# A linear-attention and expert kernel: attention units overlapped three deep in a written VectorE order, with filling products on TensorE

## The chip, the core and the metric

One core of a Trainium2 chip runs the whole program. It has five engines with a queue each: TensorE (PE in the profile; its weight loads are PEld), VectorE (DVE), ScalarE (ACT), GpSimd (POOL) and SyncE (SP, which here only issues transfers). The metric is the device time of one execution in microseconds (us).

## The reference

Three stages follow one another; the token rows pass from each to the next.

```python
# 1  attention: 4 batches x 8 heads, 768 steps, head size 48
for t in range(S):
    state = alpha[t, :, None] * state + outer(k[t], v[t])
    y[t] = q[t] @ state
x = y as 3072 rows of 384
# 2  experts: each token goes to one of 8 (argmax of a normalised product with expert_emb)
expert_idx = argmax(xn @ en.T / tau);  gate_w = its softmax probability
x = gate_w * (relu(x @ w1[e]) @ w2[e])          # 384 -> 1024 -> 384
# 3  a second network on all tokens
h = x @ w_in;  out = max(0.01 * h, h) @ w_out   # 384 -> 2048 -> 384
```

## The kernel before

**Attention** works on 16 units; unit i is one batch and one pair of heads, with the heads on partitions 0 to 47 and 64 to 111 and time along the free axis, cut into 12 chunks of 64 steps. `unit(i)` does, in dependency order:

- VectorE scans alpha forward into `bc`, the decay from each chunk's start (L326); takes 12 reciprocals as seeds (L328); scans alpha backwards into `rc`, the inverse decays (L333); and multiplies k by them into `kh` (L335). GpSimd multiplies q by `bc` into `qb` (L329), ScalarE spreads the chunk decays into `en` (L331).
- TensorE transposes `kh` in six blocks (L352), which ScalarE copies to `kn` (L355); forms the scores of all chunks, `kh` with `qb` (L343); VectorE multiplies them by a triangular mask into `am` (L346).
- TensorE forms each chunk's sum of k and v (L367); VectorE scans these into the carried states `st` (L371). TensorE then adds `am` with v (values, L385) and `qb` with `st` (carried, L392) in `py`, and ScalarE copies the result rows to `xb` (L401).

**Routing** follows for each batch once its four units are done: `columns` transposes the rows (L448) and takes the products with the experts' embeddings (L460, 8 columns each), `squares` sums the squares of the rows, and `route` goes through about 25 operations on 128x6 or 128x48 tiles on VectorE, ending in `slot`. Then GpSimd scatters the batch's rows into per-expert buckets in DRAM with six indirect transfers (L532). The buckets are first cleared by `zero_rows` (L539, L540), on SP's queue. The scattered rows of the last batch are what the first expert gathers (L745).

What sets the order is the class `Plan`: every operation is added with an engine, an assumed duration, what it reads and writes, and a wish time `at`. `order` lists them greedily by assumed start, and `emit` issues them in that order, so each engine has a fixed queue and runs it strictly in order. The weights of the first expert are split into two fp16 parts in the same plan (L563 on ScalarE, L564 on VectorE). `fence` is a TensorE drain.

**The experts and the second network** (from L616 on) are not planned but written out; before the first expert, `x2h` and `x2l`, the second network's input, are set to zero by VectorE (L620) and GpSimd (L621).

## Time and profile before

| | |
|---|---|
| median of 3 runs | 897.55 us (897.52 to 908.74) |
| the profiled execution | 898.16 us, span 896.4 us |
| TensorE, VectorE, ScalarE, GpSimd busy | 782.0, 461.2, 361.1, 152.5 us |
| mean granted TensorE clock | 0.88 |
| first scan, last key product ends, last scatter begins, first expert product | 13.3, 201.4, 234.8, 253.1 us |

The span has two parts. From 13.3 to 253 us the attention and the routing run, with TensorE mostly at half of its clock; from 253 us on the products of the experts and of the second network fill TensorE at nearly its full clock. The profile gives each engine's busy time by stretch, the granted clock as a share of full speed (0.50 is 1.2 GHz, 1.00 is 2.4 GHz), and a timeline of single instructions. Ends of matrix products are modelled and overlap the next one's start, so where one row follows another directly, the step from start to start is the better price.

### The profile page before, as it was taken

Reading aid. Unit: us, or ns where it says so; the run is one execution under the profiler, and the core shown is the slowest. Engines: PE = TensorE matmul, PEld = TensorE weight load, DVE = VectorE, ACT = ScalarE, POOL = GpSimd, SP = SyncE. Lnnn points to the kernel's source line nnn. Section 1 sums busy time; section 2 is a strip of 40 time slices with the busy share of each in tenths; the row PEclk is TensorE's granted clock in tenths of the full one; section 3 lists DMA queues with packets and bytes.
Section 4 is the critical chain, followed back from the end, with each engine's and each line's share of the span. In section 5 each row is a group of like instructions: output and inputs, shape, how many; then the busy total and the mean of one; then the engine's idle time right before and its main releaser. Section 6 shows DMA issues by size and latency. Waiting matters only on the chain.

```text
span 896.4 us, 17082 instructions
## 1 busy us (share of the span) xinstructions
PE 782.0 (87%) x7172; PEld 476.2 (53%) x7172; DVE 461.2 (51%) x748; ACT 361.1 (40%) x661; POOL 152.5 (17%) x130
## 2 busy tenths in 40 slices
PE   1839989889288798788698999999999999999996
PEld 1738878788244344344354445545546446455453
DVE  5668686781356666665667673062260350540620
ACT  2235242422136665765666343152251340531520
POOL 3011231212313222322324000100000001001001
PEclk9656576665579899999899999999999999999999
DMA  9975453201275859768766000000000000000000
GB/s 309 329 251 167 130 179 108 93 2 55 71 194 174 167 138 228 168 149 235 153 156 207 15 2 10 27 1 18 19 1 19 18 1 27 10 10 24 3 10 28
DMA packets 63729, 87.56 MB, mean 98 GB/s; under 512 B 29848, under 2 KB 42912, under 8 KB 63648
## 3 DMA queue, kind: packets, MB, share of 16 engines
q1 hardware_dynamic: 41472, 72.27, 28.3%
q10 hardware_dynamic: 19040, 4.65, 3.1%
q0 software_dynamic: 3136, 9.50, 2.8%
q8 instruction: 58, 0.95, 0.5%
q14 instruction: 23, 0.19, 0.1%
HBM read 66.85 MB, written 14.91 MB: 91 GB/s over the span
## 4 chain that ended last, share of the span: by engine, by line
issue 40%; PE 24%; DVE 13%; DMA 12%; ACT 6%; POOL 4%; ACTq 1%; SPq 0%; POOLq 0%; DVEq 0%
DMA wstage<-in_w_out 5%; DMA xt<-xs 4%; PE py L385 4%; PE pkv L367 3%; PE pkv L460 3%; POOL out L728 3%; PE py L392 2%; PE ptr L352 2%; PE psc L343 2%; ACT wstage L187 2%; DVE t L641 2%; PE ptr L448 1%; DVE w2l L194 1%; DVE rc L333 1%; ACT w2h L189 1%
## 5 line engine op out<-in xcount | busy, mean ns | idle before, releaser
L711 DVE SCALAR_TENSOR_TENSOR g<-ps,r 128x512 f32<-128x512 f32 x96 | 65.7, 685 | 150.3 <-ACT r L710 150.3
L723 PE MATMUL ps<-woh,gh 128*128 128x384 f16 x384 | 125.2, 326 | 0.0
L725 PE MATMUL ps<-woh,gl 128*128 128x384 f16 x384 | 125.2, 326 | 0.0
L724 PE MATMUL ps<-wol,gh 128*128 128x384 f16 x384 | 125.2, 326 | 0.0
L705 PE MATMUL ps<-x2h,wih 128*128 128x512 f16 x288 | 109.2, 379 | 0.0
L707 PE MATMUL ps<-x2h,wil 128*128 128x512 f16 x288 | 109.2, 379 | 0.0
L706 PE MATMUL ps<-x2l,wih 128*128 128x512 f16 x288 | 109.2, 379 | 0.0
L715 DVE TENSOR_TENSOR gl<-g,gh 128x512 f16<-128x512 f32 x96 | 66.5, 693 | 64.1 <-ACT gh L714 64.0
L714 ACT ACTIVATE gh<-g 128x512 f16<-128x512 f32 x96 | 60.4, 630 | 83.8 <-DVE g L711 83.8
L695 PE MATMUL ps<-hl,w2h 128*128 128x432 f16 x192 | 69.7, 363 | 15.4 <-DVE hl L686 15.3
L728 POOL DMA_INDIRECT out<-osb,tki x24 | 23.3, 971 | 350.9 <-ACT osb L727 344.1
L680 PE MATMUL ps<-xt,w1h 128*128 128x432 f16 x192 | 67.5, 351 | 12.5 <-DVE hl L686 12.1
L727 ACT ACTIVATE osb<-ps,ms 128x384 f32<-128x384 f32 x24 | 13.9, 580 | 159.5 <-PE ps L725 159.5
L694 PE MATMUL ps<-hh,w2h 128*128 128x432 f16 x192 | 69.6, 363 | 8.1 <-ACT hh L685 7.9
L696 PE MATMUL ps<-hh,w2l 128*128 128x432 f16 x192 | 69.6, 362 | 0.0
L681 PE MATMUL ps<-xt,w1h 128*128 128x432 f16 x192 | 67.5, 351 | 0.1
L682 PE MATMUL ps<-xt,w1l 128*128 128x432 f16 x192 | 67.4, 351 | 0.0
L710 ACT ACTIVATE r<-ps 128x512 f32<-128x512 f32 x96 | 55.9, 582 | 8.3 <-PE ps L707 8.3
L352 PE MATMUL ptr<-ident,kh 128*128 128x128 f32 x96 | 23.3, 409 | 35.2 <-DVE kh L335 34.6
L192 POOL TENSOR_TENSOR w1l<-wstage,w1h 128x768 f16<-128x768 f32 x21 | 34.7, 1653 | 109.6 <-ACT w1h L189 109.6
L724 PEld LDWEIGHTS <-gh 128*128 128x128 f16 x384 | 37.6, 98 | 25.1
L723 PEld LDWEIGHTS <-gh 128*128 128x128 f16 x384 | 37.6, 98 | 25.1
(181 smaller groups left out, 1293.1 us busy)
## 6 DMA issues: line engine op xcount, KB each, us to landing
wstage<-in_w SPq DMA_DIRECT2D x64, 384.0 KB, 5.1
a<-in_aT SPq DMA_DIRECT2D x16, 390.5 KB, 3.4
q<-in_qT SPq DMA_DIRECT2D x16, 384.0 KB, 4.2
k<-in_kT SPq DMA_DIRECT2D x16, 384.0 KB, 5.3
wstage<-in_w_in SPq DMA_DIRECT2D x16, 384.0 KB, 3.1
wstage<-in_w_out SPq DMA_DIRECT2D x16, 384.0 KB, 5.2
bucket<-zero SPq DMA_DIRECT2D x8, 582.0 KB, 7.8
v<-in_v SPq DMA_DIRECT2D x8, 576.0 KB, 8.8
```

The costliest lines, as they stand in the source:

```text
L680: nc.tensor.matmul(ps, w1h[:, k, fs], xth[:, k], start=k == 0, stop=False)
L681: nc.tensor.matmul(ps, w1h[:, k, fs], xtl[:, k], start=False, stop=False)
L682: nc.tensor.matmul(ps, w1l[:, k, fs], xth[:, k], start=False, stop=k == KD - 1)
L694: nc.tensor.matmul(ps, w2h[:, f, dsl], hh, start=f == 0, stop=False)
L695: nc.tensor.matmul(ps, w2h[:, f, dsl], hl, start=False, stop=False)
L696: nc.tensor.matmul(ps, w2l[:, f, dsl], hh, start=False, stop=f == NF1 - 1)
L705: nc.tensor.matmul(ps, wih[:, k, fs], xh[:, k], start=k == 0, stop=False)
L706: nc.tensor.matmul(ps, wih[:, k, fs], xl[:, k], start=False, stop=False)
L707: nc.tensor.matmul(ps, wil[:, k, fs], xh[:, k], start=False, stop=k == KD - 1)
L723: nc.tensor.matmul(ps, ghs[f][:, ts], woh[:, f], start=f == 0, stop=False)
L724: nc.tensor.matmul(ps, ghs[f][:, ts], wol[:, f], start=False, stop=False)
L725: nc.tensor.matmul(ps, gls[f][:, ts], woh[:, f], start=False, stop=f == NF2 - 1)
```

## The change

`unit(i)` is taken apart into `front` (scans, key product, query product, transposes), `score`, `mask_scores`, `middle` (values, then sums) and `back` (state scan, carried, rows). One round of the loop puts down the front and the scores of unit i, the mask of unit i-1, the back of unit i-2 and the middle of unit i-1. `in_turn` chains these VectorE operations, so the planner can't reorder them among each other. The scaled query no longer has a tile: it is written over `rc` after the key product has read it, so it waits for that product; `rc` and `en` have three buffers. Two drains per unit are gone. The last unit's query product is on VectorE, and its result stands in the scores' bank.

`emit` now puts products of 512 columns of ones (`keep_busy`) wherever the plan leaves TensorE a gap, into a bank that is free then; 15 stand ahead of everything. 73 more are in gaps.

The routing of a batch is spread over three rounds; that of the third batch is put behind the last unit, as are the last four weight pieces. The squares of the last batch are summed on VectorE in three parts. Only rows 256 to 431 of each expert's bucket are cleared, later; `x2h` and `x2l` are not cleared. The loads' order changes with the plan.

```diff
-    HOP = 0.2
+    HOP, TAIL = 0.07, {"PE": 0.2}
...
+    def add(self, eng, us, fn, reads=(), writes=(), pe=(), ps=(), lock=False, at=None, size=0, after=()):
+        deps = {self.wrote[k] for k in after}
...
+    def emit(self, keep=None, banks=(), us=0.22, share=0.6):
...
+        pe = [i for i in order if self.ops[i][0] == "PE"]
+        for i, j in zip(pe, pe[1:]):
+            t0, t1 = self.start[i] + self.ops[i][1], self.start[j]
...
+            if free:
+                t0, b = min(free)
+                due += [(t0 + n * us, 0, lambda b=b: keep(b)) for n in range(int((t1 - t0) * share / us + 0.4))]
+        for _, _, fn in sorted(due, key=lambda d: d[:2]):
+            fn()
...
+        tbc, trc = tiles_of("bc", [AW], 2), tiles_of("rc", [AW], 3)
+        tkh, tam = tiles_of("kh", [S], 2), tiles_of("am", [2, NC, CL], 2)
+        tkn, ten, tst = tiles_of("kn", [NC, P], 2), tiles_of("en", [HD, NCL], 3), tiles_of("st", [HD, NCL], 2)
...
+        busy = tiles_of("busy", [512], 1, F16)[0]
+        nc.vector.memset(busy, 1.0)
...
-            plan.add(G_, 1.76, lambda: nc.gpsimd.tensor_tensor(chunks(qb), chunks(q), bcv[:, :, 1:W], op=ALU.mult),
-                     [("q", i % 3), ("bc", i % 2)], [("qb", i % 3)], lock=True)
...
+        def in_turn(us, fn, reads, writes, ps=(), lock=False):
+            plan.add(V, us, fn, reads, writes, ps=ps, lock=lock, after=["turn"] if "turn" in plan.wrote else ())
+            plan.wrote["turn"] = len(plan.ops) - 1
...
+        def front(i):
+            a, q, k = ta[i % 3], tq[i % 3], tk[i % 3]
+            bc, rc, kh, kn, en = tbc[i % 2], trc[i % 3], tkh[i % 2], tkn[i % 2], ten[i % 3]
+            bcv, rcv = chunks(bc, 0, W), chunks(rc, 1, W)[:, :, 1:]
+            in_turn(1.76, lambda: nc.vector.tensor_tensor_scan(bc, a, onesP, 0.0, op0=ALU.mult, op1=ALU.add), [("a", i % 3)], [("bc", i % 2)], lock=True)
+            in_turn(0.2, lambda: nc.vector.reciprocal(seeds[:, W::W], bcv[:, :, CL]), [("bc", i % 2)], ["seeds"])
...
+            in_turn(1.76, lambda: nc.vector.tensor_tensor_scan(rc[:, ::-1], a[:, ::-1], seeds[:, ::-1], 0.0, op0=ALU.mult, op1=ALU.add),
+                    [("a", i % 3), "seeds"], [("rc", i % 3)], lock=True)
+            in_turn(0.94, lambda: nc.vector.tensor_tensor(chunks(kh), chunks(k), rcv, op=ALU.mult), [("k", i % 3), ("rc", i % 3)], [("kh", i % 2)], lock=True)
+            if i < NU - 1:
+                plan.add(G_, 1.76, lambda: nc.gpsimd.tensor_tensor(rcv, chunks(q), bcv[:, :, 1:], op=ALU.mult),
+                         [("q", i % 3), ("bc", i % 2)], [("rc", i % 3)], lock=True)
+            else:
+                in_turn(0.94, lambda: nc.vector.tensor_tensor(rcv, chunks(q), bcv[:, :, 1:], op=ALU.mult), [("q", i % 3), ("bc", i % 2)], [("rc", i % 3)], lock=True)
...
+                            nc.tensor.matmul(psc[CL * p:CL * p + CL, j, cp * CL:(cp + 1) * CL], kh[r, t], rcv[r, 2 * cp + p], start=True, stop=True)
+            plan.add(T_, 0.7, scores, [("kh", i % 2), ("rc", i % 3)], ["sc"], pe=SCB)
...
+        def part_squares(b, h, n, row):
+            x, w = txb[b % 3][:, :, 2 * h * HD:2 * (h + n) * HD], late[:, :, :2 * n * HD]
+            small(S_, lambda: nc.scalar.activation(w, x, AF.Square), [("xb", b % 3, u, g) for u in range(h, h + n) for g in range(2)], ["late"], 0.2 + 0.48 * n)
+            small(V, lambda: nc.vector.tensor_reduce(tsm[b % 2][:, row], w, AX.X, ALU.add), ["late"], [("part", h)], 0.1 + 0.6 * n)
...
-                         [("bucket", b, c)], size=P * AUG * 4, lock=True)
+                         [("bucket", b, c)], size=P * AUG * 4)
...
-                nc.sync.dma_start(bucket[e * NT:e * NT + 384].rearrange("(n p) d -> p n d", p=P), zero.unsqueeze(1).to_broadcast([P, 3, AUG]))
-                nc.sync.dma_start(bucket[e * NT + 384:e * NT + CAP], zero[:CAP - 384])
-            plan.add(Q_, 0.16, go, [], [("zeroed", e)], size=CAP * AUG * 4)
+                nc.sync.dma_start(bucket[e * NT + z0:e * NT + z0 + P], zero)
+                nc.sync.dma_start(bucket[e * NT + z0 + P:e * NT + CAP], zero[:CAP - z0 - P])
+            plan.add(Q_, 0.16, go, [], [("zeroed", e)], size=(CAP - z0) * AUG * 4, after=["turn"])
...
-            for i in range(NU):
+            for i in range(NU + 2):
                 plan.at = i
                 if i + 2 < NU:
                     load(i + 2)
-                unit(i)
+                if i < NU:
+                    front(i)
+                if 1 <= i <= NU:
+                    mask_scores(i - 1)
+                if i < NU:
+                    score(i)
+                if i >= 2:
+                    back(i - 2)
+                if 1 <= i <= NU:
+                    middle(i - 1)
...
-                    zero_rows(2 * i - 2)
-                    zero_rows(2 * i - 1)
+                if 2 <= i < 6:
+                    zero_rows(2 * i - 4)
+                    zero_rows(2 * i - 3)
...
-                if i >= 4 and i % 4 < 2:
-                    for c in range(3 * (i % 4), 3 * (i % 4) + 3):
-                        columns(i // 4 - 1, [c], range(KD))
-                        squares(i // 4 - 1, c)
-                    if i % 4 == 1:
-                        plan.at = i + 0.8
-                        route(i // 4 - 1, False)
-                if i == NU - 2:
+                b, step = divmod(i - 6, NP)
+                if 0 <= b < B - 1 and step < 3:
+                    for c in range(2 * step, 2 * step + 2):
+                        columns(b, [c], range(KD))
+                        squares(b, c)
+                    if step == 2:
+                        plan.at = i + 0.8 if b < B - 2 else NU + 1.2
+                        route(b, False)
+                if i == NU - 1:
+                    plan.at = NU - 0.2
+                    part_squares(B - 1, 0, 2, 0)
+                if i == NU:
+                    plan.at = NU + 0.5
                     for c in range(0, NC, 2):
                         columns(B - 1, [c, c + 1], range(KD - 1))
-                    for c in range(NC):
-                        squares(B - 1, c, 2 * (NP - 1) * HD)
+                    part_squares(B - 1, 2, 1, 11)
                     small(S_, lambda: nc.scalar.activation(lga, spare(0, 1), AF.Copy), [("dots", 1, 0, c) for c in range(NC)], ["lga"], 0.25, ps=KVB)
-                if 7 <= i < 15:
-                    convert(i - 7, *pieces[i - 7], w_first)
+                if 8 <= i < 16:
+                    plan.at = NU + 1 if i > 11 else i
+                    convert(i - 8, *pieces[i - 8], w_first)
+            plan.at = NU + 1.5
             columns(B - 1, [0, 1, 2], [KD - 1])
             columns(B - 1, [3, 4, 5], [KD - 1], V)
+            part_squares(B - 1, 3, 1, 12)
             route(B - 1, True)
-            plan.emit()
+            def keep_busy(bank):
+                nc.tensor.matmul({"s0": psc[:, 0], "t0": ptr[0], "t1": ptr[1]}[bank], ones16, busy, start=True, stop=True)
+            for _ in range(15):
+                keep_busy("s0")
+            plan.emit(keep_busy, ("s0", "t0", "t1"))
...
-    nc.vector.memset(x2h.rearrange("p k t -> p (k t)").bitcast(F32), 0.0)
-    nc.gpsimd.memset(x2l.rearrange("p k t -> p (k t)").bitcast(F32), 0.0)
```

**VectorE, a middle unit.** Before, units 4 and 5 (`bc` forward decays, `rc` inverse decays, `kh` scaled keys, `am` masked scores, `st` states, `sm` routing):

```order
L335 TENSOR_TENSOR kh_124<-k_109,rc_119 128x768
L326 SCALAR_TENSOR_TENSOR bc_117<-a_104,onesP_98 128x781
L328 RECIPROCAL seeds_99<-bc_117 128x12
L333 SCALAR_TENSOR_TENSOR rc_119<-a_104,seeds_99 128x781
L346 TENSOR_TENSOR am_126<-psc,mask_100 128x768
L371 SCALAR_TENSOR_TENSOR st_132<-pkv,en_130 128x576
L335 TENSOR_TENSOR kh_123<-k_110,rc_119 128x768
L326 SCALAR_TENSOR_TENSOR bc_118<-a_105,onesP_98 128x781
L328 RECIPROCAL seeds_99<-bc_118 128x12
L333 SCALAR_TENSOR_TENSOR rc_119<-a_105,seeds_99 128x781
L346 TENSOR_TENSOR am_125<-psc,mask_100 128x768
```

Now, the same place:

```order
L345 SCALAR_TENSOR_TENSOR bc_117<-a_104,onesP_98 128x781
L346 RECIPROCAL seeds_99<-bc_117 128x12
L349 SCALAR_TENSOR_TENSOR rc_120<-a_104,seeds_99 128x781
L351 TENSOR_TENSOR kh_122<-k_110,rc_120 128x768
L387 TENSOR_TENSOR am_125<-psc,mask_100 128x768
L425 SCALAR_TENSOR_TENSOR st_131<-pkv,en_130 128x576
L345 SCALAR_TENSOR_TENSOR bc_118<-a_105,onesP_98 128x781
L346 RECIPROCAL seeds_99<-bc_118 128x12
L349 SCALAR_TENSOR_TENSOR rc_121<-a_105,seeds_99 128x781
L351 TENSOR_TENSOR kh_123<-k_111,rc_121 128x768
L387 TENSOR_TENSOR am_124<-psc,mask_100 128x768
```

The mask stood behind the next unit's second scan or ahead of the key product, as the plan had it; now every round reads scan, reciprocal, scan, key product, mask of the unit before, states of the one before that.

**TensorE, a middle unit without routing.** Before (`ptr` transposes, `psc` scores, `pkv` sums, `py` values and carried):

```order
L352 MATMUL ptr_160<-ident,kh_124 128x128 x3
L352 MATMUL ptr_161<-ident,kh_124 128x128 x3
L343 MATMUL psc<-qb_120,kh_124 64x64 x24
L367 MATMUL pkv<-v_112,kn_128 48x24 x44
L385 MATMUL py<-v_112,am_126 64x48 x24
L392 MATMUL py<-st_132,qb_120 64x48 x22
L352 MATMUL ptr_160<-ident,kh_123 128x128 x3
```

Now (`busy` and `ones` are the filling products):

```order
L360 MATMUL ptr_160<-ident,kh_122 128x128 x3
L360 MATMUL ptr_161<-ident,kh_122 128x128 x3
L666 LDWEIGHTS ones_75
L666 MATMUL psc<-busy_175,ones_75 128x512
L666 LDWEIGHTS ones_75
L666 MATMUL psc<-busy_175,ones_75 128x512
L373 MATMUL psc<-rc_120,kh_122 64x64 x24
L432 MATMUL py<-st_131,rc_121 64x48 x22
L666 LDWEIGHTS ones_75
L666 MATMUL ptr_160<-busy_175,ones_75 128x512
```

Between the transposes and the scores stand two filling products; the carried products are of the unit two back, and behind them stand three filling products (the first is the last row here), then values and sums of the unit before. In a round with routing, its transposes and 8-column products stand there, with at most a few filling ones.

**GpSimd, the end of attention.** Before:

```order
L329 TENSOR_TENSOR qb_120<-q_106,bc_117 128x768
L329 TENSOR_TENSOR qb_121<-q_107,bc_118 128x768
L329 TENSOR_TENSOR qb_122<-q_108,bc_117 128x768
L329 TENSOR_TENSOR qb_120<-q_106,bc_118 128x768
L532 DMA bucket<-xb_116,slot_149 24576x388 x6
L532 DMA bucket<-xb_114,slot_150 24576x388 x6
L621 MEMSET x2l 128x5256
```

Now:

```order
L353 TENSOR_TENSOR rc_120<-q_107,bc_118 128x12x64
L575 DMA bucket<-xb_115,slot_150 24576x388 x6
L353 TENSOR_TENSOR rc_121<-q_108,bc_117 128x12x64
L575 DMA bucket<-xb_116,slot_149 24576x388 x6
L575 DMA bucket<-xb_114,slot_150 24576x388 x6
L209 TENSOR_TENSOR w1l<-wstage,w1h 128x768 x3
```

The last query product is gone from this queue (it is on VectorE), the second batch's scatters stand two query products later, and `x2l` is not cleared. The third and fourth batch's scatters close the attention on this queue as before.

## Rows read from the trace of the kernel before

**Rows 1.** Busy time by stretch; columns: stretch, length, five engines, PEclk, DMA, GB/s.

```profile
...
13.30:201.40 188.10, 152.54 (x3608) 137.11 (x3609) 142.82 (x173) 65.27 (x131) 38.79 (x28) 0.64 0.51 168
201.40:234.80 33.40, 26.93 (x390) 24.09 (x387) 9.75 (x39) 8.52 (x25) 5.85 (x6) 0.50 0.10 37
234.80:253.10 18.30, 2.64 (x12) 2.28 (x13) 7.55 (x14) 2.67 (x6) 10.29 (x7) 0.50 0.59 193
98.00:111.50 13.50, 13.31 (x231) 12.12 (x234) 8.05 (x21) 3.07 (x7) 3.62 (x3) 0.50 0.38 126
```

**Rows 2.** VectorE's groups, 13.3 to 201.4: line, operation, count, busy, mean ns, idle before.

```profile
...
L333 DVE TENSOR_TENSOR_SCAN rc<-a,seeds 128x781 f32<-128x781 f32 x16 | 46.2, 2888 | 0.5
L326 DVE TENSOR_TENSOR_SCAN bc<-a,onesP 128x781 f32<-128x781 f32 x16 | 28.4, 1776 | 0.0
L371 DVE TENSOR_TENSOR_SCAN st<-pkv,en 128x576 f32<-128x576 f32 x14 | 18.9, 1351 | 12.3 <-PE pkv L367 10.9 <-ACT junk L466 1.4
...
L346 DVE TENSOR_TENSOR am<-psc,mask 128x768 f32<-128x768 f32 x15 | 14.2, 948 | 21.7 <-PE psc L343 21.7
...
L503 DVE SCALAR_TENSOR_TENSOR cand<-lg,em 128x48 f32<-128x48 f32 x3 | 0.6, 208 | 0.1
```

**Rows 3.** Timeline at 182.5: start, duration, engine, line, operation, idle before.

```profile
...
182.57 1.68 POOL L329 TENSOR_TENSOR qb<-q,bc 128x768 f32<-128x768 f32 x1 [8.44 <-DVE bc L326]
182.74 3.16 DVE L333 TENSOR_TENSOR_SCAN rc<-a,seeds 128x781 f32<-128x781 f32 x1
```

**Rows 4.** Timeline at 107.4, GpSimd and VectorE.

```profile
...
107.41 1.68 POOL L329 TENSOR_TENSOR qb<-q,bc 128x768 f32<-128x768 f32 x1 [10.43 <-PE pkv L367]
107.53 1.35 DVE L371 TENSOR_TENSOR_SCAN st<-pkv,en 128x576 f32<-128x576 f32 x1
```

**Rows 5.** Timeline of TensorE, 86 to 98.

```profile
...
86.95 1.56 PE L343 MATMUL psc<-qb,kh 48*64 48x64 f32 x48
88.29 2.38 PE L367 MATMUL pkv<-v,kn 64*48 64x24 f32 x88
...
91.43 3.13 PE L385 MATMUL py<-v,am 64*64 64x48 f32 x48
94.67 1.52 PE L392 MATMUL py<-st,qb 48*64 48x48 f32 x44
96.12 1.54 PE L448 MATMUL ptr<-ident,xb 128*128 128x128 f32 x6
```

**Rows 6.** Timeline of TensorE, 174 to 184.

```profile
...
174.24 1.87 PE L385 MATMUL py<-v,am 64*64 64x48 f32 x47
...
176.69 1.24 PE L392 MATMUL py<-st,qb 48*64 48x48 f32 x44
177.86 0.87 PE L448 MATMUL ptr<-ident,xb 128*128 128x128 f32 x6
178.57 2.07 PE L460 MATMUL pkv<-enT,xt 128*128 128x8 f32 x18
180.50 0.85 PE L352 MATMUL ptr<-ident,kh 128*128 128x128 f32 x6
181.28 0.93 PE L343 MATMUL psc<-qb,kh 48*64 48x64 f32 x48
182.03 1.50 PE L367 MATMUL pkv<-v,kn 64*48 64x24 f32 x88
```

**Rows 7.** Timeline of TensorE at 600, products of 512 columns.

```profile
...
600.19 0.38 PE L707 MATMUL ps<-x2h,wil 128*128 128x512 f16 x1
600.40 0.38 PE L705 MATMUL ps<-x2h,wih 128*128 128x512 f16 x1
```

**Rows 8.** Timeline between the last scatter and the first expert.

```profile
...
236.09 0.96 POOL L532 DMA_INDIRECT bucket<-xb,slot  x1 [0.30 <-issue]
...
245.25 4.44 DVE L620 MEMSET x2h<- 128x5256 f32 x1 [8.87 <-issue]
...
247.77 0.62 ACT L664 ACTIVATE xs<-xg 128x384 f32<-128x384 f32 x1 [15.18 <-DMA xg<-bucket]
```

More of the change, by code (lines that the diff above doesn't have):

```diff
@@ L98, in order @@
             free[eng] = t + us
-            end[i] = t + us
+            end[i] = t + us + self.TAIL.get(eng, 0.0)
             if size:
@@ L117, in order @@
         return sorted(done, key=lambda i: start[i])
-    def emit(self):
-        for i in self.order():
-            self.ops[i][2]()
+    def emit(self, keep=None, banks=(), us=0.22, share=0.6):
+        order = self.order()
+        due = [(self.start[i], 1, self.ops[i][2]) for i in order]
+        held = {b: sorted([(self.start[i], "w") for i in order if b in self.ops[i][4]] + [(self.end[i], "r") for i in order if b in self.ops[i][5]]) for b in banks}
+        pe = [i for i in order if self.ops[i][0] == "PE"]
+        for i, j in zip(pe, pe[1:]):
+            t0, t1 = self.start[i] + self.ops[i][1], self.start[j]
+            free = []
+            for b in banks:
+                last = [h for h in held[b] if h[0] < t1]
+                if not last:
+                    free.append((t0, b))
+                elif last[-1][1] == "r":
+                    free.append((max(t0, last[-1][0] + 0.1), b))
+            if free:
[3 more added lines that the diff above has]
+            fn()
 BLK = 512
@@ new lines, in middle, with values @@
+        def middle(i):
+            b, hp = divmod(i, NP)
+            vt, am, kn = tv[b % 2], tam[i % 2], tkn[i % 2]
+            _, key, banks = result(i)
+            def values():
+                for cp in range(NC):
+                    for j in range(2):
+                        for p in range(2):
+                            r, e0 = slice(CL * p, CL * p + CL), (2 * hp + j) * HD
+                            nc.tensor.matmul(y_of(i, 2 * cp + p, j), am[r, j, cp], vt[r, cp, e0:e0 + HD], start=cp == 0, stop=False)
+            plan.add(T_, 1.4, values, [("am", i % 2), ("v", b % 2, hp // 2)], [key], pe=banks)
```

117 lines of the change are left out of this document (47 added, 70 removed).

## The prediction

> **What bounds the kernel now.** I read the busy time by stretch first [rows 1]. The reader is to see three stretches ahead of the experts: 188.1 us from the first scan to the last key product, 33.4 us to the last batch's scatter, 18.3 us to the first expert product. In the first one VectorE works 142.8 us and TensorE 152.5, and neither sets the pace alone: VectorE stands still for 188.1 - 142.8 = 45.3 us, and its groups say for what [rows 2]: 21.7 us at the mask for the scores, 10.9 at the state scan for the sums, both TensorE's. TensorE is late because its granted clock is 0.64 there and 0.50 in the next stretch [rows 1]. So I read TensorE's timeline at both levels. At 1.2 GHz one unit takes 1.54 (transposes; the same six as the routing's row), 1.34 (scores, start to start), 2.38 (sums), 3.24 (values), 1.45 (carried) = 9.95 us [rows 5]. At 2.4 GHz it takes 0.78 + 0.75 + 1.50 + 1.87 + 1.17 = 6.07 us [rows 6]. The second loss is on VectorE itself: the backward scan takes 2.89 us in the mean, the forward one of the same size 1.78 [rows 2]. The timeline shows why: GpSimd's query product starts 0.17 us ahead of the backward scan, runs 1.68, and the scan lasts 3.16 [rows 3].
>
> Everything behind the first expert product is unchanged, so the sum needs only those three stretches. It is made against the profiled execution, 898.16 us, which is 0.6 us above the median of the runs shown.
>
> **First stretch, VectorE.** The query product now follows the key product, so beside it run the mask and the state scan. A state scan beside that very GpSimd product took 1.35 us, as its mean, and the product its 1.68 [rows 4, 2]: no price. A mask beside it is in no row; bounds are nothing (the state scan's row) and a full block of 1.68 per unit; I take nothing, since it reads PSUM as the state scan does. So 16 x (2.888 - 1.776) = 17.8 us go. Up to the last key product VectorE also loses one mask (0.95), one state scan (1.35), four low weight parts (128x768 as the mask, 0.95 each) and some 24 routing operations of 0.21 [rows 2] to the last stretch: 11.1 us. 142.8 - 17.8 - 11.1 = 113.9; the ends of these operations overlap a little, so less than their means go, and I take 116, or 7.25 per round.
>
> **First stretch, TensorE.** If it held 2.4 GHz: 15 units x 6.07 = 91; 14 routing groups of three transposes (half of 0.71) and three products (0.107 each) = 9.5 [rows 6]; 64 filling products in that stretch at 0.21, the step of two products of 512 columns [rows 7] = 13.4. Together 114 us, just under VectorE's 116. At 1.2 GHz: 15 x 9.95 = 149; 14 x (0.77 + 0.64, doubling the products) = 20; 64 x 0.42 = 27; together 196 us, far over it. Two drains a unit are gone, which I don't deduct. So the clock decides, and the filling products are what the change offers for it.
>
> Which level will it be? From 98.0 to 111.5 TensorE was busy 13.31 of 13.50 us, and the clock stayed at 0.50 [rows 1]; from 174 to 183 it ran at its full level through transposes, scores, values, carried and sums [rows 6]. Being occupied is thus not enough, and the attention's own products can hold the level once it is there. Products of 512 columns stand now between these in seven rounds of sixteen; in the nine routing rounds hardly any do. I expect the full level in the plain rounds and lapses in routing rounds. The Trainium skill ("TensorE: Matmul & The Clock Gate", What's actually happening) says that the slow level is the default and activity releases it. By that rule rounds without idle time would not lapse and the sum would be 8 us lower; this case's trace disagrees with it at 98 to 111.5, so I keep the lapses.
>
> **Waits left in the first stretch**, between nothing and today's 45.3; I take 15. Nine routing rounds have 6.07 + 1.36 + 0.2 = 7.6 us of TensorE against 7.0 to 7.3 of VectorE, about 5 in all. Two lapsed rounds at 9.95 + 1.4 = 11.4 cost 8. The start and hand-overs cost 2. The clearing on SP's queue, its weight loads and the reordered loads cost nothing: a unit's tiles are loaded three rounds ahead, and a transfer share of 0.51 leaves room in that stretch [rows 1]; if that cover failed, the first scan of a round would wait for alpha.
>
> So the last key product ends at 13.3 + 116 + 15 = 144.3 instead of 201.4: 57.1 us.
>
> **Second stretch.** From that product on, the chain is: query product 0.95 on VectorE, mask 0.95, state scan 1.35, carried 1.2, ScalarE's copy of the rows 0.7 (an estimate: a tile of 576 columns by the mask's 0.95 for 768), values and sums of unit 14 (1.9 + 1.5), values of 15 (1.9), six transposes 0.7, sums 1.5: about 13 us; state scan 15 to 14.4; the rest of the carried products, the fourth batch's transposes and products with ScalarE's copies between, to 18.6; copy, the third batch's ranks, its slots at about 20.6; its six scatters, from 21.4, at 0.96 + 0.30 each [rows 8] to 29.0. The fourth batch's slots are ready at about 26, but stand behind those scatters. So 29 us instead of 33.4: 4.4 us. Bounds: 26 with no scatters in the way, 37 if TensorE's 12.5 us of it run at 9.95 / 6.07 of that.
>
> **Third stretch.** The gathered rows are there at 247.77, when ScalarE starts on its block; VectorE is still clearing `x2h`, which began at 245.25 and takes 4.44 [rows 8]. Without it VectorE's block starts 1.9 us sooner, and TensorE's first transposes wait for that one. GpSimd's clearing hides nothing.
>
> **Sum:** 57.1 + 4.4 + 1.9 = 63.4; 898.2 - 63.4 = **835 us**.
>
> **Rivals.**
> 1. *Lapses in most rounds.* For it: the clock's mean of 0.64 and the stretch at 98 [rows 1]. Against it: the filling products. With half of TensorE's work at each level it has (114 + 196) / 2 = 155 us from the first key product's end (18.0) plus 5 of waits, so 178 instead of 201.4; the next stretch comes to 33, and 1.9 go: 898.2 - 23.4 - 0.4 - 1.9 = 872 us.
> 2. *Slower than before: the filling products don't lift the clock and are dead weight.* Place: every round's TensorE queue, where in-order work stands behind them. 18.0 + 196 = 214 is 12.6 later, the tail 37 instead of 33.4, 1.9 go: 912 us. It decides once TensorE's round passes 188.1 / 16 = 11.8 us, against 11.7 to 13 at the slow level with filling. Against it: the rise before 174 came without any filling product [rows 6].
> 3. *The fixed order hands waits around.* The state scan of one unit releases carried, copy, values, sums and so the next state scan: 1.35 + 1.17 + 1.87 + 1.50 = 5.9 [rows 2, 6], with the copy and hand-overs 7 to 8.7 against 7.25. At the upper end 16 x 1.7 us would come on top of the forecast's stretch: 862. For it: VectorE already waits 10.9 us at that scan. Against it: it now has a round more to wait in.
> 4. *GpSimd's scatters amid scans.* In the first stretch 12 scatters now meet dense scans. No row here shows such a pair undisturbed or disturbed. As a mechanism: if each waited for a scan's 1.78 [rows 2], two batches of 7.6 + 10.7 us would hold up the next query products by two rounds, some 16 us: 851. The Trainium skill ("SBUF — State Buffer", SBUF: two separate sides) says that transfers issued by GpSimd can't write their descriptors while VectorE holds the shared port pair; which scans hold it, no run here shows.
>
> **Chances and range.** Forecast 0.60 (its own range 818 to 850), rival 1 0.18, rival 2 0.08, rival 3 0.10, rival 4 0.04. A measurement of this kernel can tell about 2% from no change: under 879.6 is faster, over 915.5 slower. Rival 1 reaches past 879.6 in a fifth of its cases, rival 2 past 915.5 in a third. Faster 0.89, same 0.08, slower 0.03. The range holds the forecast, rivals 3 and 4 and half of rival 1: 814 to 874.
>
> **What would show it.** Right: the last key product near 144, backward scans at 1.78, VectorE's idle time in that stretch near 15, a granted clock of 0.9 or more there, the fourth batch's scatters right behind the third's, the first expert product near 190. Wrong: masks or scans lengthened beside the query product; granted clock near 0.7; VectorE waiting more than 1 us a round for the sums; a first scan that waits for alpha.

## The result, and the profile after

The changed kernel takes 860.48 us (median of 4 runs, 858.25 to 865.45) against 901.03 for the kernel before on the same chip: ratio 0.955, 95% interval 0.946 to 0.963. The profiled execution takes 858.25 us, its span is 856.5. The forecast was 835, so 40 us came where 63 were expected. First the same stretches as [rows 1] in the changed kernel (the bounds are the first scan, the end of the last key product, the fourth batch's first scatter, the first expert product; columns as there):

```profile
15.10:158.10 143.00, 122.95 (x3371) 100.99 (x3371) 119.25 (x144) 59.32 (x121) 45.10 (x27) 0.86 0.61 194
158.10:204.70 46.60, 42.03 (x700) 37.77 (x698) 23.24 (x78) 12.55 (x26) 5.85 (x6) 0.57 0.07 23
204.70:221.20 16.50, 3.02 (x13) 2.05 (x14) 2.08 (x5) 2.81 (x6) 5.80 (x6) 0.50 0.56 188
221.20:856.50 635.30, 598.08 (x3168) 312.37 (x3167) 297.69 (x509) 282.31 (x494) 93.60 (x69) 0.98 0.31 76
```

| us | before | forecast | after | after against forecast |
|---|---|---|---|---|
| first scan starts | 13.3 | 13.3 | 15.1 | +1.8 |
| to the last key product's end | 188.1 | 131.0 | 143.0 | +12.0 |
| to the fourth batch's first scatter | 33.4 | 29.0 | 46.6 | +17.6 |
| to the first expert product | 18.3 | 16.4 | 16.5 | +0.1 |
| to the end | 643.3 | 643.3 | 635.3 | -8.0 |

The second stretch became longer than before, and the experts, where nothing was forecast, gave 8 us. The first stretch on VectorE (line, operation, count, busy, mean ns, idle before and its releaser), against [rows 2]:

```profile
L349 DVE TENSOR_TENSOR_SCAN rc<-a,seeds 128x781 f32<-128x781 f32 x16 | 30.5, 1908 | 10.4 <-PE py L432 9.4
L345 DVE TENSOR_TENSOR_SCAN bc<-a,onesP 128x781 f32<-128x781 f32 x16 | 29.1, 1819 | 0.0
L425 DVE TENSOR_TENSOR_SCAN st<-pkv,en 128x576 f32<-128x576 f32 x13 | 17.6, 1353 | 10.0 <-PE pkv L499 5.6 <-PE pkv L416 4.3
L387 DVE TENSOR_TENSOR am<-psc,mask 128x768 f32<-128x768 f32 x14 | 13.3, 950 | 0.0
```

Backward scans fell from 2888 to 1908 ns, masks and state scans kept their length beside the query product, the 21.7 us of waiting at the mask are gone. New is the backward scan's wait of 9.4 us for the carried products: its tile, three deep, is free only when the unit three before is finished with it.

TensorE's clock in 40 slices, before and then after:

```profile
PEclk9656576665579899999899999999999999999999
```

```profile
PEclk8999958555799899999999999999999999999999
```

One slice is 22.4 us before and 21.4 after. After, the clock is full from 23.5 to 105 us and then half for most of the time to 200. The first fall stands behind a row of six scatters. GpSimd's timeline there (the last three of the six, then the query product) and TensorE's:

```profile
100.14 0.97 POOL L575 DMA_INDIRECT bucket<-xb,slot  x1 [0.30 <-DVE kh L351]
101.41 0.96 POOL L575 DMA_INDIRECT bucket<-xb,slot  x1 [0.30 <-PE ptr L360]
102.68 1.19 POOL L575 DMA_INDIRECT bucket<-xb,slot  x1 [0.30 <-issue]
103.88 2.32 POOL L353 TENSOR_TENSOR rc<-q,bc 128x768 f32<-128x768 f32 x1
```

```profile
102.28 1.24 PE L432 MATMUL py<-st,rc 48*64 48x48 f32 x44
106.25 1.56 PE L373 MATMUL psc<-rc,kh 48*64 48x64 f32 x48 [2.74 <-POOL rc L353]
107.74 1.45 PE L499 MATMUL pkv<-enT,xt 128*128 128x8 f32 x6
109.11 2.69 PE L401 MATMUL py<-v,am 64*64 64x48 f32 x45
...
152.45 1.56 PE L373 MATMUL psc<-rc,kh 48*64 48x64 f32 x48 [4.29 <-POOL rc L353]
```

The key product was there at 100; the query product stood in GpSimd's queue behind three scatters until 103.88. TensorE stood idle 2.74 us, the clock fell at 105.5, and scores take 1.56 and values 2.69 us instead of 0.93 and 1.54. The second batch's scatters do the same ahead of 152.45; there the clock fell at 149.8, within the wait. The two falls between, at 122.5 and 136.2, have no such wait: TensorE was idle for 0.12 us or less of the 4 us before each, and what lost the level there stays open.

### The profile page after: what moved, and what is told of

It is laid out like the page before. It is cut to its first block, busy times and chain, and to the rows that moved or that the text cites. A ratio compares the mean times of both kernels' runs of the same rounds, so it can differ in the third digit from the quotient of the medians.

```text
span 856.5 us, 17230 instructions
## 1 busy us (share of the span) xinstructions
PE 772.4 (90%) x7260; PEld 455.3 (53%) x7260; DVE 446.6 (52%) x752; ACT 359.3 (42%) x651; POOL 154.3 (18%) x129
## 4 chain that ended last, share of the span: by engine, by line
issue 39%; DMA 12%; PE 11%; DVE 9%; POOL 5%; ACT 4%; SPq 1%; ACTq 0%; POOLq 0%; DVEq 0%
DMA wstage<-in_w_out 5%; DMA meta<-xg 3%; POOL out L793 3%; DVE t L706 2%; DMA xt<-xs 2%; ACT wstage L204 2%; ACT w2h L206 2%; DVE w2l L211 1%; PE pkv L499 1%; DVE t L708 1%; PE ps L771 1%; PE ps L770 1%; PE ps L772 1%; DVE t L707 1%; DMA wstage<-in_w 1%
## 5 line engine op out<-in xcount | busy, mean ns | idle before, releaser
L745 PE MATMUL ps<-xt,w1h 128*128 128x432 f16 x192 | 68.9, 359 | 17.7 <-DVE hl L751 17.3
L760 PE MATMUL ps<-hl,w2h 128*128 128x432 f16 x192 | 67.8, 353 | 9.5 <-DVE hl L751 9.5
L759 PE MATMUL ps<-hh,w2h 128*128 128x432 f16 x192 | 67.8, 353 | 2.5 <-ACT hh L750 2.5
L746 PE MATMUL ps<-xt,w1h 128*128 128x432 f16 x192 | 69.0, 359 | 0.0
L761 PE MATMUL ps<-hh,w2l 128*128 128x432 f16 x192 | 67.8, 353 | 0.0
L790 PEld LDWEIGHTS <-gl 128*128 128x128 f16 x384 | 37.6, 98 | 24.8
```

The costliest lines, as they stand in the source:

```text
L745: nc.tensor.matmul(ps, w1h[:, k, fs], xth[:, k], start=k == 0, stop=False)
L746: nc.tensor.matmul(ps, w1h[:, k, fs], xtl[:, k], start=False, stop=False)
L759: nc.tensor.matmul(ps, w2h[:, f, dsl], hh, start=f == 0, stop=False)
L760: nc.tensor.matmul(ps, w2h[:, f, dsl], hl, start=False, stop=False)
L761: nc.tensor.matmul(ps, w2l[:, f, dsl], hh, start=False, stop=f == NF1 - 1)
L790: nc.tensor.matmul(ps, gls[f][:, ts], woh[:, f], start=False, stop=f == NF2 - 1)
```

## Experiments

Each kernel's ratio is to the kernel before on the same chip. The kernel before differed from chip to chip (901 to 925 us), so ratios of different groups are compared with care, and stages are read from each one's profile. "Falls" are times between the first scan and the last key product's end at which the granted clock goes from full to half; the one behind the 15 opening products (at 11 to 15 us in most kernels) is left out. "Issue" in a view means that the profile names nothing for which the engine waited.

**Scatters spread.** Two or four scatters behind a query product instead of six ahead of one, for the first two batches.

```diff
-plan.add(G_, 1.1, scatter, reads, [("bucket", b, c)], ...)
+if b < B - 2: later.append((scatter, reads, [("bucket", b, c)]))
...
+for scatter, reads, writes in later[:2]:      # once a round
+    plan.add(G_, 1.1, scatter, reads, writes, ..., after=["product"])
```

> The changed kernel (858.25 us in its profiled execution, last key product at 158.1) with the first two batches' scatters spread on GpSimd's queue, two or four behind a query product instead of six ahead of one. Theory A, six scatters in a row hold up the query product, TensorE stands idle for it (2.74 us before 106.25, 4.29 before 152.45), and the granted clock falls and stays low: both waits go, the granted clock stays at 0.9 or more up to the last key product, that product ends near 147, the tail runs partly at the full level, and the time is 832 to 846 us. Theory B, rounds with routing lose the clock by themselves because their products are few and small: the clock from 107 to 158 stays near 0.7, the last key product moves by less than 3 us, the time is 853 us or more.

Measured: 855.62 us, ratio 0.942 [0.932, 0.952]. TensorE's waits for the query product went from 7.6 to 0.6 us, and from 108 to 162 us the clock is at 1.00. The last key product ends at 154.3. But it fell at 56.9, 80.7 and 101.2 instead, and at 162.7, so the time lies in Theory B's range, and the ratio is not told apart from the changed kernel's 0.955. A's mechanism is borne out at its two places by these two profiles; it is not the only way to lose the clock.

**The other falls.** In this kernel TensorE stands still in the middle of a group of products, with "issue" as the reason. Its timeline from 45 us:

```profile
45.17 0.56 PE L433 MATMUL py<-st,rc 48*64 48x48 f32 x15 [1.04 <-issue]
45.66 0.82 PE L676 MATMUL ptr<-busy,ones 128*128 128x512 f16 x3
46.48 1.54 PE L402 MATMUL py<-v,am 64*64 64x48 f32 x46
47.81 0.23 PE L417 MATMUL pkv<-v,kn 64*48 64x24 f32 x2
47.86 0.22 PE L402 MATMUL py<-v,am 64*64 64x48 f32 x2
47.88 1.22 PE L417 MATMUL pkv<-v,kn 64*48 64x24 f32 x59
50.55 0.54 PE L417 MATMUL pkv<-v,kn 64*48 64x24 f32 x27 [1.46 <-issue]
51.02 0.87 PE L361 MATMUL ptr<-ident,kh 128*128 128x128 f32 x6
51.73 0.59 PE L676 MATMUL psc<-busy,ones 128*128 128x512 f16 x2
52.25 0.93 PE L374 MATMUL psc<-rc,kh 48*64 48x64 f32 x48
53.00 1.22 PE L433 MATMUL py<-st,rc 48*64 48x48 f32 x44
54.15 0.39 PE L676 MATMUL ptr<-busy,ones 128*128 128x512 f16 x1
56.47 0.67 PE L676 MATMUL ptr<-busy,ones 128*128 128x512 f16 x2 [1.93 <-issue]
```

Counted between two such waits: 15 + 3 + 46 + 2 + 2 + 59 = 127 records and 27 + 6 + 2 + 48 + 44 + 1 = 128. Each has a weight load of its own, so 256 instructions. In the changed kernel the waits at 40.21, 44.76 and 49.05 lie as far apart. Behind the one at 56.47 the clock fell; the fall at 101.2 has 0.1 us of idle time in the 4 us before it, so these waits do not account for it.

The trace also holds the transfers of a queue that the profile calls "instruction" (its row in section 3 of the changed kernel's page: packets, MB, share of 16 engines):

```profile
q8 instruction: 59, 0.97, 0.5%
```

These are 59 transfers of 16 KB. In the twelve profiles with the new order, TensorE has 57 unnamed waits of 0.5 us or more between the first scan and the last key product; 53 of them end 1.2 to 1.5 us after one of these transfers has landed. The transfer ahead of 56.47 took 3.09 us, those ahead of 45.17 and 50.55 took 0.93 and 1.00. So these are waits for a block of instructions, as far as times can show it.

**No filling.**

```diff
-for _ in range(15):
-    keep_busy("s0")
-plan.emit(keep_busy, ("s0", "t0", "t1"))
+plan.emit()
```

> The changed kernel without any of its filling products (neither the 15 ahead nor those in TensorE's gaps). Theory A, the filling products hold the clock: it falls in most rounds, the last key product ends at 175 or later (158.1 with them), the time is 872 to 905 us. Theory B, the deeper pipeline and the fixed VectorE order alone keep TensorE's gaps short enough, the filling products are idle weight: the clock up to 104 stays above 0.9 and the time is within 5 us of 858.

Measured: 871.63 us, ratio 0.958 [0.947, 0.968], not told apart from the changed kernel's 0.955; what the filling is worth is read from the stretch here, and from the ratios of the last pair below. The last key product comes at 174.2 (158.1 with filling, 166.2 in a second execution). Both figures lie just under Theory A's, and its mechanism does not hold: there are only three falls, but the first low stretch lasts from 35.4 to 110.5.

**Filling alone**, in the kernel before, with `emit`'s filling as in the change.

```diff
-            plan.emit()
+            for _ in range(15):
+                keep_busy("s0")
+            plan.emit(keep_busy, ("s0", "t0", "t1"))
```

> The kernel before with the filling products alone (15 ahead and those in the planned gaps of TensorE). Theory A, filling lifts the clock whatever the order is: mean granted clock of the first stretch 0.64 to over 0.85, TensorE's waits go, the collisions of the scans stay: 868 to 885 us. Theory B, without the deeper pipeline TensorE still stands idle where VectorE is late, in gaps that the plan does not know of, and the clock falls as before: 890 to 905 us. Theory C, dead weight at the slow level: 905 us or more.

Measured: 896.32 us, ratio 0.982 [0.973, 0.992], in the range of B and within 2% of no change. The first stretch of this kernel, and of the one without filling:

```profile
14.10:202.50 188.40, 170.24 (x3691) 140.38 (x3693) 142.66 (x173) 65.33 (x131) 38.80 (x28) 0.67 0.51 166
```

```profile
14.90:174.20 159.30, 135.31 (x3373) 123.84 (x3376) 122.30 (x144) 60.52 (x122) 42.76 (x27) 0.68 0.56 174
```

Against 188.1 before [rows 1]: filling alone 188.4, the rest of the change alone 159.3, both 143.0 (151.5 in a second execution). The rest of the change carries 29 us at nearly the same clock (0.68 against 0.64); filling needs it to be worth anything in that stretch. That rest is the deeper pipeline, the written order, fewer drains and the spread routing together; apart from the query product's place, below, no run separates them.

**The query product untied**, in a tile of its own and beside the backward scan again.

```diff
-nc.gpsimd.tensor_tensor(rcv, chunks(q), bcv[:, :, 1:], op=ALU.mult)        # behind the key product
+nc.gpsimd.tensor_tensor(chunks(qb), chunks(q), bcv[:, :, 1:], op=ALU.mult) # behind the forward scan
```

> The changed kernel with the query product in a tile of its own again, issued as soon as the forward scan is done, so beside the backward scan. Theory A, VectorE sets the pace of the rounds and the collision with the backward scan is its price: that scan goes from 1.91 us in the mean back to 2.7 or more, the last key product comes 12 to 16 us later, the time is 870 to 875 us. Theory B, the rounds are paced by TensorE's products and their chain with the state scan, so longer scans fill time in which VectorE waits, and the scores, no longer behind a held-up query product, start on time: the time is within 5 us of 858, or up to 10 us less where the two lapses of the clock go.

Measured: 859.42 us, ratio 0.944 [0.935, 0.954]. Its first stretch and two VectorE groups there:

```profile
14.30:164.10 149.80, 126.76 (x3433) 101.10 (x3434) 134.03 (x146) 60.03 (x121) 43.40 (x27) 0.85 0.58 187
```

```profile
L353 DVE TENSOR_TENSOR_SCAN rc<-a,seeds 128x781 f32<-128x781 f32 x16 | 39.4, 2462 | 0.6
L355 DVE TENSOR_TENSOR kh<-k,rc 128x768 f32<-128x768 f32 x16 | 20.8, 1300 | 0.5
```

VectorE works 134.0 us instead of 119.3: 8.9 more in backward scans and 5.5 more in key products (958 to 1300 ns), together near the forecast's 17.8. But its waits shrink from 23.8 to 15.8, and the time is not told apart from the changed kernel's. That is Theory B: the collisions fill time in which VectorE would wait. The edit also lets the scores start sooner, so the price of the collisions by themselves is not shown.

**The changed kernel again**, unchanged.

> The changed kernel itself once more, so that the others of this group stand beside it on one chip. If the falls of the granted clock hang on the program's own waits, they come at the same places as in the first profile (near 105 and near 150, behind the two rows of six scatters), and the ratio to the kernel before is 0.945 to 0.965. If they come by chance, at least one of these two places keeps the full level.

Measured: 857.66 us, ratio 0.931 [0.925, 0.937] (the kernel before is slower on this chip, so the ratio left its range). The clock fell beside both rows of scatters, at 113.5 and 157.8, but also at 52.0, 79.3, 130.5 and 144.2. TensorE's idle time there is another one than in the first execution:

```profile
113.61 1.16 PE L416 MATMUL pkv<-v,kn 64*48 64x24 f32 x44 [3.55 <-issue]
157.96 1.16 PE L416 MATMUL pkv<-v,kn 64*48 64x24 f32 x44 [4.26 <-issue]
```

It stands between the two halves of the sums, where the program has a drain (L408), and not ahead of the scores. The drain took 3.77 and 4.46 us here and at most 0.66 in the first execution; an instruction transfer had landed 3 to 4 us before its end, so it is not one of the waits above, and what it waited for stays open. In the kernel with the clearing put back (below) it is the query product again, 2.73 and 4.27 us. So an idle time beside each row of scatters comes back, as do the falls there; that the query product is its cause holds for the first execution and not for this one. The other falls change with the execution.

The last key product comes at 166.2, then 33.0 us pass to the fourth batch's scatter instead of 46.6; the clock was full from 161 to 188:

```profile
166.24:199.26 33.02, 27.44 (x644) 23.35 (x632) 23.22 (x78) 11.97 (x26) 5.87 (x7) 0.89 0.09 33
```

The four runs of this group order by the mean clock (854.5 us at 0.939, 855.9 at 0.930, 859.5 at 0.927, 861.8 at 0.923); those of the first group do not (860.98 at 0.916, 865.45 at 0.923).

**Filling among the routing products**, on top of the spread scatters.

```diff
 nc.tensor.matmul(spare(part, b % 2)[:, c], txt[m][:, s], enT[:, k], ...)
+if s % 3 == 2 or s == len(todo) - 1:
+    nc.tensor.matmul(ptr[n], ones16, busy, start=True, stop=True)
```

> The kernel with spread scatters (849.6 us of span in its profile; its clock fell at 56, 80, 101 and 162, the last two without an idle gap of 1 us, 1 to 3 us behind a run of twelve routing products of 8 columns) with one filling product of 512 columns behind every three routing products, in all four batches. Theory A, runs of these small products lose the clock as idle time does: the falls at 101 and 162 go, the tail from 156 to the last rank product runs mostly at the full level and takes 24 to 28 us instead of 36, and the time is 8 to 14 us under that kernel's, a ratio to the kernel before of 0.925 to 0.935. Theory B, only idle time loses it: the falls stay or move, TensorE's routing rounds get 0.4 to 0.9 us longer, and the time is 0 to 8 us over that kernel's.

Measured: 863.73 us, ratio 0.931 [0.920, 0.941]. That lies in Theory A's range, but the changed kernel has the same ratio on this chip. The last key product comes at 171.2, 17 us later than in the kernel with spread scatters; there are five falls, all with 0.7 us or more of idle TensorE in the 4 us before, and one low from 80.8 to 111.6. In the tail the clock is full from 173.0 to 203.7, as Theory A says, but from the last key product to the last rank product it takes 33.6 us (39.4 in the kernel with spread scatters) and not 24 to 28. By the falls it is Theory B: filling there prevents none.

**Third batch in two rounds.**

```diff
-    for c in range(2 * step, 2 * step + 2):
+    for c in range(n * step, n * step + n):    # n = 3 for the third batch, else 2
...
-        plan.at = i + 0.8 if b < B - 2 else NU + 1.2
+        plan.at = i + 0.8
```

> The changed kernel with the third batch's columns gathered in two rounds of three instead of three rounds of two, so that its rank products stand ahead of the fourth batch's transposes and routing products in TensorE's order and not behind them. Theory A, the tail is long because the third batch's slots come late (196.0) and its six scatters stand ahead of the fourth batch's: the third batch's first scatter starts 10 us or more sooner after the last key product than now (39.0 us), the fourth batch's scatters start as soon as its slots are there, and the last scatter is issued 3 to 6 us sooner after the last key product than now (53.0 us). Theory B, TensorE's work at the half level sets the tail alone: the last scatter comes within 2 us of 53 us after the last key product.

Measured: 858.55 us, ratio 0.930 [0.924, 0.937]. GpSimd's timeline, first and last of the third batch and first of the fourth:

```profile
182.24 1.01 POOL L575 DMA_INDIRECT bucket<-xb,slot  x1 [26.90 <-ACT xt L492]
...
188.66 0.97 POOL L575 DMA_INDIRECT bucket<-xb,slot  x1 [0.31 <-issue]
200.16 0.97 POOL L575 DMA_INDIRECT bucket<-xb,slot  x1 [10.53 <-issue]
```

The third batch's scatters start 19.3 us after the last key product instead of 39.0 and are out of the way, as A says. The last scatter ends after 44.5 us (54.0 in the first execution of the changed kernel, 40.4 in the second): between these, so two executions of one program differ more than this order does.

**Clearing put back.**

```diff
+nc.vector.memset(x2h.rearrange("p k t -> p (k t)").bitcast(F32), 0.0)
+nc.gpsimd.memset(x2l.rearrange("p k t -> p (k t)").bitcast(F32), 0.0)
```

> The changed kernel with the clearing of x2h (VectorE) and x2l (GpSimd) put back ahead of the experts. Both theories expect 1 to 2.5 us more between the fourth batch's first scatter and the first expert product (16.4 us without it, 17.0 before). Theory A, the clearing also held up GpSimd's and VectorE's work on the next expert's weights, and that is the 5 to 8 us by which the experts' stage became shorter (643.3 us before, 635.3 to 638.5 in five kernels without the clearing): the experts' stage is back at 641 to 645 us and the time is 6 to 10 us over the changed kernel's, a ratio to the kernel before of 0.955 to 0.965 where the latter has 0.93 to 0.955. Theory B, the stage is shorter for another reason (a different phase of weight loads and VectorE's work): it stays at 635 to 639 us and the time is within 3 us.

Its runs lie between 851 and 870 us, too far apart for a ratio; the stages are read from its profile. From the fourth batch's first scatter (212.62) to the first expert product (230.85) it takes 18.2 us, against 16.4 without clearing and 18.3 before (not 17.0): 1.8 us, where the prediction had 1.9. The experts' stage stays at 637.2: Theory B.

**Clearing of the buckets later.**

```diff
-if 2 <= i < 6:
-    zero_rows(2 * i - 4)
-    zero_rows(2 * i - 3)
+if 5 <= i < 9:
+    zero_rows(2 * i - 10)
+    zero_rows(2 * i - 9)
```

> The changed kernel with the clearing of the buckets' rows on SP's queue three rounds later. TensorE's idle times for which the profile names no cause lie 128 matmuls apart (40.21, 44.76, 49.05, 56.94 in the changed kernel, 0.37 to 1.04 us each; 0.65 to 1.93 in the kernel with spread scatters, where the clock then fell at 56.9). Theory A, they are waits for the next block of instructions behind other transfers: with fewer transfers from 30 to 60 us (their share 0.83 to 0.93 there now) their sum between 24 and 66 us falls from 2.6 to 7 us to under 1.5 us, they grow between 70 and 100 us, and the clock does not fall before 75. Theory B, they have nothing to do with the transfers: their sum between 24 and 66 us stays at 2.5 us or more. The time moves by less than 1% under either.

Measured: 860.2 us, ratio 0.946 [0.936, 0.955]. The unnamed waits from 24 to 66 us still sum to 3.1 us (0.70, 1.31, 0.83, 0.25), and the first fall is at 67.6. Theory B by its number: this clearing is not what lengthens them. What makes a block late stays open.

**Three edits together**: scatters spread, third batch in two rounds, the embeddings' norm behind the first units' scans.

```diff
-small(S_, lambda: nc.scalar.activation(..., accum_out=ess[:, 0:1]), [], ["ess", ("junk", 0)], 0.7)
+plan.add(S_, 0.7, lambda: nc.scalar.activation(..., accum_out=ess[:, 0:1]), [], [...], after=["turn"])
```

> The changed kernel with spread scatters, the third batch's columns in two rounds of three, and the embeddings' norm behind the second unit's scans instead of ahead of the first scan in VectorE's order. If VectorE's order is what starts the first scan late (15.09 in the changed kernel; the first alpha was there 5.4 us after its issue at 0.80), the first scan starts at 7 to 9 us and the last key product comes 5 to 7 us sooner than in the kernel with spread scatters alone (154.3), at 147 to 150; with the tail's 2 to 4 us from the earlier third batch the time is 838 to 849 us, a ratio to the kernel before of 0.915 to 0.930. If the first rounds are held by the loads of keys and queries instead, the last key product stays within 2 us of 154 and the time is 848 to 856 us.

Measured: 842.2 us, ratio 0.929 [0.916, 0.942]. The first scan starts at 4.6 us, the last key product ends at 145.7. With either of the other two edits alone the first scan starts at 14.8 and 14.0, so the norm's place is what moved it: VectorE's written order had held the first scan behind a load for the embeddings. The changed kernel's VectorE, whose first alpha was there at 3.95 (the 5.4 us are a median of three loads):

```profile
12.96 0.14 DVE L454 TENSOR_SCALAR ess<-ess 8x1 f32<-8x1 f32 x1 [8.68 <-ACT junk L463]
...
15.09 1.77 DVE L345 TENSOR_TENSOR_SCAN bc<-a,onesP 128x781 f32<-128x781 f32 x1
```

**More filling, and none, on that kernel.**

```diff
-def emit(self, keep=None, banks=(), us=0.22, share=0.6):
+def emit(self, keep=None, banks=(), us=0.22, share=1.0):
```

> The best kernel so far (spread scatters, third batch in two rounds, late norm of the embeddings: 835.6 us of span, last key product at 145.7) with TensorE's planned gaps filled wholly instead of to 0.6 (131 instead of 80 filling products behind the first 15). Theory A, more filling holds the clock longer: fewer falls than six before the last key product, which ends at 138 to 143, time 3 to 8 us less. Theory B, the falls come behind waits that the plan doesn't know (blocks of instructions, a late query product), which no planned filling covers, and each filling product adds two instructions to the stream: the falls stay at five or more, the time is within 4 us of that kernel's or up to 6 us more.

> The same kernel without any filling product. Theory A, filling is worth what it was in the changed kernel (there the last key product came 8 to 16 us later without it): the last key product ends at 153 to 165, the clock is at the half level for 60 us or more before it, the time is 848 to 862 us. Theory B, with the other waits gone the attention's own products hold the clock as well as with filling: the time is within 4 us.

Measured: 838.62 us, ratio 0.918 [0.912, 0.925] with more, 864.41, 0.949 [0.941, 0.957] with none. The first stretch at a share of 0.6, at 1.0 and without filling:

```profile
4.60:145.70 141.10, 128.18 (x3447) 101.82 (x3448) 119.96 (x151) 60.68 (x126) 43.34 (x27) 0.89 0.66 216
```

```profile
4.50:150.50 146.00, 132.20 (x3475) 102.76 (x3477) 119.71 (x151) 60.55 (x126) 42.74 (x28) 0.93 0.65 211
```

```profile
4.20:164.30 160.10, 136.02 (x3297) 124.23 (x3298) 120.55 (x153) 61.09 (x125) 41.48 (x29) 0.66 0.59 195
```

| kernel | filling | falls | us at the half level behind them | longest |
|---|---|---|---|---|
| before | none | 6 | 134 | 41 |
| before | 0.6 | 5 | 103 | 38 |
| changed | 0.6 | 4 | 32 | 14 |
| changed, again | 0.6 | 6 | 38 | 17 |
| changed | none | 3 | 102 | 75 |
| three edits | 0.6 | 5 | 31 | 10 |
| three edits | 1.0 | 5 | 20 | 7 |
| three edits | none | 4 | 109 | 34 |

For more filling Theory B holds as to the falls (five), and its intervals overlap those at 0.6; for none Theory A holds, 2 us above its range. On one chip, the ratios with full filling and with none (0.918 and 0.949) have intervals that do not meet: filling is worth 3% there. In the new order there are no fewer falls with filling, but each is over sooner: the half level behind them sums to 20 to 60 us in the ten profiles with filling, to 102 and 109 in the two without. In the old order it goes from 134 to 103 us only. The two filled kernels are the fastest here, 7 to 8% under the kernel before.

## Why the prediction was right, and where it was off

The time fell inside the range (814 to 874) and outside the likeliest case's own (818 to 850); the sum was 23 us too low, and its terms did not all hold. In part it is luck: the experts gave 8 us that no term had, and without them the miss would be 31 us, still inside the range.

- **Backward scans without the query product: right in size, wrong in worth.** 1908 ns against 1.78 us forecast; fourteen of the sixteen take 1.78, and two ran beside a query product (2.81 at 21.9, beside the first unit's, and 2.74 at 105.09, beside one that stood behind scatters). The mask and the state scan beside the product cost nothing (950 and 1353 ns). But having the product beside the scan again cost VectorE 14.7 us and the kernel nothing measurable: VectorE did not set the pace alone.
- **VectorE's work and waits.** 119.3 us of work against 116; 23.8 of waits against 15. With the later first scan (1.8) this is the 13.8 us by which the last key product is late. The late start is no chance: the embeddings' norm stands ahead of the first scan, as before, and its load landed later. The last of the combined edits removed it. Among the waits is a term that the forecast lacks: TensorE's unnamed waits sum to 5.6 us in that stretch, and to 13.6 in the second execution.
- **The clock, mis-argued.** The forecast had the filling hold the full level in plain rounds and lose it in routing rounds. Measured, the first stretch has 0.86 (0.9 forecast) and falls come in both kinds of rounds. Filling does not prevent them; in the new order it shortens the low stretches (table above). The Trainium skill ("TensorE: Matmul & The Clock Gate", What's actually happening) has activity release the level; that filling ends low stretches agrees, but being occupied was not enough: in the three edits without filling TensorE was busy 33.60 of 34.00 us at a clock of 0.50 (busy time of one stretch, columns as above):

```profile
66.00:100.00 34.00, 33.60 (x682) 31.17 (x684) 22.54 (x27) 12.74 (x25) 4.56 (x3) 0.50 0.41 124
```

- **The second stretch: the step that failed.** The forecast put 12.5 us of TensorE's work on that chain and bounded it by 37 us at the half level. TensorE is busy 42.0 of 46.6 us there at 0.57, with 700 products where the kernel before had 390 [rows 1]: all its work counts, the third batch's last two chunks and the fourth batch's transposes and routing products too. At a higher clock it took 33.0 us (the changed kernel again, 0.89) and 33.2 (untied, 0.85); even in the first of these TensorE is busy 27.4 us, over twice the 12.5. By the two executions of one program, 4 us of the miss are the chain and 13.6 the level, an estimate.
- **Third stretch: right,** 16.4 (204.74 to 221.16) against 16.4, and 18.2 with the clearing back.
- **Rivals.** Rival 1 (lapses in most rounds, 872) is nearest in kind, but the low time is 32 us, not half the stretch. Rival 2 is refuted: the kernel is faster than before, and without filling the best kernel is slower. Rival 3's chain shows in VectorE's waits, 9.4 us for carried products and 4.3 for sums (5.6 more are for routing products), some of them in low stretches. Rival 4's place was right and its price wrong: the scatters take 7.6 and 9.2 us for six instead of 5.8 to 6.0, but the harm is the query product behind them, at most 4.3 us a row and not a round, and the clock that falls. Which operations lengthen a scatter the runs do show (last section).
- **Not seen: the experts, 8 us.** In all twelve profiles with the new attention that stage takes 635 to 640 us, with the old 643.3 and 645.0. The removed clearing is not the cause, and filling isn't either. TensorE's waits for ScalarE's half of the hidden rows went from 7.9 to 2.5 us, those for VectorE's from 27.4 to 26.8; but with the clearing back the first are 6.2 and the stage is as short. Why stays open.

## What to carry to other kernels

When an engine's clock depends on what it did before, price a stall twice: the idle time, and the work behind it at the lower level; behind a 2.7 us wait stood 14 us at the half level here. Look at every queue between producer and consumer for batches of transfers ahead of the one operation that the pace hangs on, and spread them; here that took the wait from 7.6 to 0.6 us, though the time moved too little to tell. Filler work was worth placing only after the order was right; whether to fill the gaps wholly or to 0.6 is not told apart here.

## What the runs showed of the hardware

- Of 54 falls of TensorE's clock before the last key product in the twelve profiles with the new order, 47 (87%) have at least 0.5 us of idle TensorE in the 4 us before; seven have 0.4 or less. Of stretches of 4 us with the clock full throughout, 28% have as much. So falls go with idle time, but not every idle time is followed by a fall (1.04 us at 44.76 in the changed kernel was not), and for seven it does not account.
- TensorE waited 0.2 to 3.2 us at places 256 of its instructions apart, mostly before 90 us, where transfers are dense (a share of 0.73 from 24 to 90 us of the changed kernel, 0.47 from 90 to 158), and 53 of the 57 unnamed waits of 0.5 us or more end 1.2 to 1.5 us after a 16 KB instruction transfer has landed. The Trainium skill ("Runtime: NRT & Kernel Launch", Instruction fetch mechanics) says that instructions come in blocks of 256 and that crossing a block is mostly hidden; the spacing agrees, the hiding does not in these rows. Why some blocks come late is not shown.
- A scatter alone takes 0.97 us to issue; beside VectorE's forward and backward scans and key products, which read and write no PSUM, it takes up to 2.5 (1.83 at 98.00, 2.48 at 141.23). Beside a mask or a state scan, which read PSUM, it takes 0.96 to 1.01 (100.14, 101.41 and 139.92).
- The same kernel before took 901 to 925 us in the medians of five groups of runs, the changed one 858 and 860 in two.
